# Attention and token/channel mixer on one core: k, q, v order for two groups of early loads, and projections of keys and values as two steps there

## The chip, the cores and the metric

The kernel runs on one core of one Trainium2 chip. The metric is the device time of one execution in microseconds (us). Three runs of the kernel before gave 423.52, 423.50 and 422.79 us; the median is 423.5 us. The profiled execution took 423.1 us by the same clock, and its profile spans 421.2 us from the first to the last instruction. All times within the profile count from its start.

## What is computed

The reference is a Linformer attention over batch 8, 8 heads, sequence 1024 and head width 64, whose result goes through one MLP-Mixer block. E and F are both 64 x 1024 and shorten keys and values from 1024 to 64 rows.

```python
k_proj = einsum('ks,bhsd->bhkd', E, k)
v_proj = einsum('ks,bhsd->bhkd', F, v)
attn   = softmax(q @ k_proj^T / sqrt(64))          # 1024 x 64 per head
x      = (attn @ v_proj), heads side by side       # 8 x 1024 x 512
h      = relu(x^T @ w_tok1) @ w_tok2               # token mixing, 1024 -> 256 -> 1024
u      = x + h^T
out    = u + relu(u @ w_ch1) @ w_ch2               # channel mixing, 512 -> 1536 -> 512
```

The inputs and the output are float32; the kernel works in bfloat16 and accumulates in float32.

## The kernel before

Work goes by batch. For each batch there is a **front**: the projections of keys and values, the scores, softmax and attention, then token mixing, which leaves u. After it come two **channel blocks** j = 2b and 2b + 1 of 512 rows each. A channel block has an up part (L1144, three sets m) and a down part (L1253); both use seven products where eight would be usual, so VectorE makes sums and differences beside TensorE. The front of batch b + 1 is woven into the channel blocks of batch b, so that TensorE always has channel work to do while the attention's small steps wait for ScalarE and VectorE. Batch 0 has nothing to hide behind, so its front is done by head pairs (hp = 0 to 3). Batch 1's front is done in two halves of four heads, A and B. Later batches take all eight heads at once.

Nothing of the weaving is written out by hand. Each step is a job of class Planner with an engine, a cost, what it reads and writes, the PSUM bank that it takes, and a due time (prio). plan() works through them greedily, and the instructions are then emitted in the order that it found. Each engine runs its own list in that order, and an instruction that waits holds up everything behind it on its engine. A small change in costs or due times can therefore move instructions all over the program. Where plan() expects TensorE to be idle at the start, the last loop of the kernel puts in blank matmuls on zeros (L405), which keep the array at work and compute nothing.

The steps of a front that matter here:

- load_heads (its DMA is issued at L346): one load of k, v or q for some heads from HBM, converted to bfloat16 on the way, always from GpSimd's queue. For batch 0 it is called per head pair in the order k, v, q, for batch 1 per half in the order k, v, q, from the literal "kvq".
- kv_proj (L484 and L487): 16 matmuls, eight of E with keys into rows 0 to 63 of a PSUM bank and eight of F with values into rows 64 to 127, in turns. They are one job, so none is issued ahead of the arrival of both k and v. ScalarE then copies keys (into wS, L506) and values (into vb, L506) out of the bank.
- k_transpose (L533) turns the projected keys on TensorE, with copies into kT at L544 and L549. q_transpose_pe (L581) turns q for batches 0 and 1, with the copy into qT at L589. From batch 2 on, DMA transposes on SyncE's queue do both (L516, L562).
- scores (L597), exponentials on ScalarE (L606), attend (L620), division by the row sums on VectorE (L632, L637).
- token1_pair (L1032), token2_pair (L1059, with the VectorE add at L1071) and u_transpose_pe (L1085, copies at L1091) mix tokens of batch 0. For batch 1 these are token1 (L687) and token2 (L711, with the add at L722). From batch 1 on, a DMA transpose per half of the rows makes uT from u (L759).
- The sums S at L781 need all of a uT half. With them the up part of a channel block can begin in earnest.

Loads of later batches and the transposes of u take turns. load_kv(b) ties the loads of k and of the first half of v of batch b behind the transpose of the first half of u of batch b - 2, the transpose of its second half behind that load of v, and the second load of v behind that transpose:

```python
jobs = load_group(b, "kv", first)
if second:
    tie(second, jobs[2])
    tie(jobs[3], second)
```

For b = 3 the cycle is thus: first half of u of batch 1, its transpose, loads k, k, v, transpose of the second half of u, last load v, kv_proj of batch 3.

Of the kernel before, what the change touches and what calls it, by code (L numbers as in the profile page):

```python
# [11 lines left out]
ALU = mybir.AluOpType  # L12
ACT = mybir.ActivationFunctionType
EARLY = 12.0
WHOLE = 3
TWO = 2
SUMS = 60.0
# [181 lines left out]
def kernel(  # L199
# [13 lines left out]
    nc = tc.nc  # L213
    P = 128

    B, H, S, D = q.shape
    KP = E.shape[0]
# [4 lines left out]
    NSI = S // P  # L222
# [37 lines left out]
    def bank(b):  # L260

        return banks[b.at] if b.span == 1 else psum[:, b.at : b.at + 2]
# [7 lines left out]
    k_sb, v_sb, q_sb = [tile_of([P, H, NSI, D], BF16, f"{n}_sb") for n in "kvq"]  # L270
# [11 lines left out]
    vb = tile_of([P, H, 2, D1], BF16, "vb")  # L282
# [48 lines left out]
    def act(cols, fn, **kw):  # L331
        t = cols / 1200 + 0.07
        return pl.add("ACT", t, t + 0.105, fn, **kw)
# [30 lines left out]
    for hp in range(HP):  # L364
        if hp == HP - 1:
            w1t = moe_w_tok1.rearrange("(p si) t -> p si t", p=P)
            ld(1.05, dma(wt1_sb, w1t), writes=["wt1"], prio=next(first))
        for name in "kvq":
            load_heads(0, name, 2 * hp, 2, next(first))
    w2t = moe_w_tok2.rearrange("(tc p) s -> p tc s", p=P)  # L370
    ld(1.05, dma(wt2_sb, w2t), writes=["wt2"], prio=next(first))
# [53 lines left out]
    for n, (src, dst) in enumerate(((EF[1], FT_sb), (EF[0], ET_sb))):  # L425
        b = Bank("S", full=False)

        def view(b=b):
            return bank(b).rearrange("p (si k) -> p si k", si=NSI)
# [41 lines left out]
    def kv_proj(b, h0, hn, due, block=False):  # L471
        hs = slice(h0, h0 + hn)
        hk = slice(h0 % (H // 2), h0 % (H // 2) + hn)
        heads = range(h0, h0 + hn)
        bk = Bank(stream[0], full=False)

        def view():
            return bank(bk).rearrange("p (h d) -> p h d", d=D)

        def mm(lo, hi):  # L480
            t = view()
            for si in range(lo, hi):
                a, z = si == 0, si == NSI - 1
                nc.tensor.matmul(  # L484
                    t[0:KP, 0:hn], ET_sb[:, si, :], k_sb[:, hs, si, :], start=a, stop=z
                )
                nc.tensor.matmul(  # L487
                    t[KP : 2 * KP, 0:hn], FT_sb[:, si, :], v_sb[:, hs, si, :], start=a, stop=z
                )

        cols = hn * D
        reads = ["ET", "FT"] + [(n, h) for n in "kv" for h in heads]
        pl.add(
            "PE", 8 * max(cols, 128) / 2400 + 0.22, 8 * max(cols, 128) / 2400 + 0.22,
            lambda: mm(0, NSI), reads=reads, takes=[bk], prio=due,
            after=[("vb", i, h) for i in range(2) for h in heads],
        )
        src = [lambda: view()[0:KP, 0:hn], lambda: view()[KP : 2 * KP, 0:hn]]
        if block:
            k_to = [kb[i * KP : (i + 1) * KP, hs, i, :] for i in range(2)]  # L500
        else:
            k_to = [kp[:, hk, i, :] for i in range(2)]
        v_to = [vb[i * KP : (i + 1) * KP, hs, i, 0:D] for i in range(2)]

        def copy(to, n):
            return lambda: nc.scalar.copy(out=to, in_=src[n]())  # L506

        for i in range(2):
            act(cols, copy(k_to[i], 0), writes=[("kb" if block else "kp", i, h if block else h % (H // 2)) for h in heads], uses=[bk])
        for i in (1, 0):  # L510
            act(cols, copy(v_to[i], 1), writes=[("vb", i, h) for h in heads], uses=[bk])

    def k_transpose_dma():
        sp(
# [56 lines left out]
    def q_transpose_pe(hp, due):  # L571
        bk = Bank(stream[0], full=False)

        def view():
            return bank(bk).bitcast(BF16).rearrange("p (h j s) -> p h j s", h=2, j=NJ)

        def mm():
            t = view()
            for h in range(2):
                for j in range(NJ):  # L580
                    nc.tensor.transpose(  # L581
                        t[:, h, j, :],
                        q_sb[:, 2 * hp + h, 2 * j : 2 * j + 2, :].rearrange("p s d -> p (s d)"),
                        ident,
                    )

        pe(2 * NJ, 128, mm, reads=[("q", 2 * hp), ("q", 2 * hp + 1)], takes=[bk], prio=due)
        act(
            1024, lambda: nc.scalar.copy(out=qT[:, 2 * hp : 2 * hp + 2], in_=view()),  # L589
            writes=[("qT", 2 * hp), ("qT", 2 * hp + 1)], uses=[bk],  # L590
        )
# [782 lines left out]

    for hp in range(HP):
        due = -26.0 + 3.9 * hp
        kv_proj(0, 2 * hp, 2, due)
        k_transpose(2 * hp, 2, due + 1)
        q_transpose_pe(hp, due + 1.5)
        for h in (2 * hp, 2 * hp + 1):  # L1380
            scores(h, due + 2)
        for h in (2 * hp, 2 * hp + 1):
            for half in range(2):
                attend(h, half, due + 3)
# [24 lines left out]
    def front(b, begin, end):  # L1409
        units = []  # L1410

        def unit(cost, f):
            units.append((cost, f))

        hn = H // 2 if b == 1 else H
        for i in range(H // hn):
            if b == 1:
                unit(1.9 * hn / H, lambda t, i=i: kv_proj(b, i * hn, hn, t))
                unit(0.9 * hn / H, lambda t, i=i: k_transpose(i * hn, hn, t))
            else:  # L1420
                unit(1.9, lambda t: kv_proj(b, 0, H, t - EARLY, True))
                unit(0.0, lambda t: k_transpose_dma())
            if b == 1:
                for hp in range(2 * i, 2 * i + 2):
                    unit(0.4, lambda t, hp=hp: q_transpose_pe(hp, t))
        if b + 1 < B:
            unit(0.0, lambda t: load_kv(b + 1))
        unit(0.4, lambda t: scores(0, t))
        unit(0.4, lambda t: scores(1, t))
        for h in range(H):  # L1430
            if h + 2 < H:
                unit(0.4, lambda t, h=h: scores(h + 2, t))
            if b >= WHOLE:
                unit(0.5, lambda t, h=h: attend_whole(h, t))
                continue
            for half in range(2):
                unit(0.25, lambda t, h=h, half=half: attend(h, half, t))
        if b < 2:
            for n in range(TC):
                unit(1.8, lambda t, n=n: token1(n, t))  # L1440
        else:
            unit(3.2, lambda t: token1_seven(b, t))
        if b < 3:
            for si in range(NSI):
                unit(0.55, lambda t, si=si: token2(b, si, t))
        else:
            unit(4.0, lambda t: token2_seven(b, t))
        total = sum(c for c, _ in units)
        done = 0.0
        for c, f in units:  # L1450
            f(begin + (end - begin) * done / total)
            done += c

    for hh in range(0, H, H // 2):
        for name in "kvq":
            load_heads(1, name, hh, H // 2, next(first))
    for b in range(B):
        for j in (2 * b, 2 * b + 1):
# [68 lines left out]
```

## Time and profile before

| view | what it says |
|---|---|
| time, 3 runs | 422.79 to 423.52 us, median 423.5 |
| span of the profile, mean granted TensorE clock | 421.2 us, 1.00 |
| head of the program, 0 to 36 us | TensorE is busy 31.9 us, much of it with blanks; VectorE is busy 8.84 of the 9 us from 27 to 36 |
| 47 to 75 us | TensorE is busy all 28 us |
| loads on GpSimd's queue (q0) | 34,944 packets, 45.09 MB, 54.5% of 16 engines' span |
| DMA transposes on SyncE's queue (q1) | 61,056 packets, 16.00 MB, 21.6% |

The page shows the DMA engines nearly always busy in the first 70 us (nine tenths in the slices up to there) and TensorE nearly always busy from the second slice on. The landing of a load is its issue plus the time that the tile view gives; for the loads of the first batches the table has them.

| load | issued, us | landed, us |
|---|---|---|
| batch 0, last head pair: k, v, q | 9.41, 10.66, 11.94 | 21.25, 22.53, 23.81 |
| batch 1, half A: k, v, q | 30.86, 32.22, 33.53 | 44.86, 47.45, 49.95 |
| batch 1, half B: k, v, q | 34.92, 36.77, 38.72 | 52.49, 55.03, 57.62 |
| batch 3: k, k, v, then the last v | 85.50, 86.24, 87.40, 101.96 | 92.04, 94.54, 97.14, 107.72 |

A row of the timeline or of the groups gives start, length, engine, line, operation, and the tiles written and read; in brackets is the idle time of the engine before it and what ended that.

### The profile page before, as it was taken

The numbers are of one execution on the slowest core, as the hardware profiler recorded it, in microseconds if no ns is written. First come the engines' busy times: TensorE is split into PE (matmuls) and PEld (weight loads), VectorE is DVE, ScalarE is ACT, GpSimd is POOL, SyncE is SP. The second block draws the span as 40 slices with busy tenths as digits, with TensorE's granted clock in tenths as the row PEclk, the third lists the DMA queues.
The fourth block names the chain that finished last, engine by engine and source line by source line (L and its number), as shares of the span: only waits on it lengthen the run. The fifth ranks groups of instructions, "written<-read, shape, count | busy, mean of one in ns | idle before, by whom it ended". The sixth has DMA issues, their size and how long they took to land.

```text
span 421.2 us, 9421 instructions
## 1 busy us (share of the span) xinstructions
PE 412.1 (98%) x3838; PEld 347.7 (83%) x3838; DVE 348.0 (83%) x747; ACT 231.8 (55%) x444; POOL 66.2 (16%) x104
## 2 busy tenths in 40 slices
PE   7999999999999999999999999999999999999996
PEld 3587877688788888888798888888898899988885
DVE  2359969679679798988889899898988798997685
ACT  1858884475636546564645556655646645354530
POOL 8453220022003030022103020212100000010110
PEclk9999999999999999999999999999999999999999
DMA  9999999996975989398974989999760501250223
GB/s 166 207 201 206 207 206 164 225 177 140 216 145 103 195 133 235 64 186 141 207 163 94 191 139 224 163 200 179 153 146 0 152 27 76 50 151 2 102 100 103
DMA packets 96668, 62.48 MB, mean 148 GB/s; under 512 B 62064, under 2 KB 92272, under 8 KB 96624
## 3 DMA queue, kind: packets, MB, share of 16 engines
q0 software_dynamic: 34944, 45.09, 54.5%
q1 hardware_dynamic: 61056, 16.00, 21.6%
q10 hardware_dynamic: 624, 0.79, 0.7%
q8 instruction: 30, 0.49, 0.5%
q14 instruction: 14, 0.11, 0.1%
HBM read 59.24 MB, written 16.78 MB: 180 GB/s over the span
## 4 chain that ended last, share of the span: by engine, by line
PE 91%; DVE 4%; ACT 2%; DMA 1%; issue 0%; DVEq 0%
PE psum L1253 34%; PE psum L1144 33%; PE psum L848 4%; PE psum L484 4%; PE psum L597 3%; PE psum L964 3%; PE psum L656 2%; DMA o<-in_F_dram 1%; PE psum L620 1%; DVE u L1071 1%; PE psum L736 1%; PE psum L687 1%; PE psum L581 1%; PE psum L405 1%; PE psum L711 1%; PE psum L1032 1%
## 5 line engine op out<-in xcount | busy, mean ns | idle before, releaser
L1253 PEld LDWEIGHTS <-G 128*128 128x128 bf16 x1344 | 130.6, 98 | 19.7 <-issue 1.5
L1253 PE MATMUL psum<-wc_sb,G 128*128 128x256 bf16 x768 | 102.5, 273 | 0.5 <-ACT psum L1309 0.2
L1166 ACT ACTIVATE G<-psum 128x512 bf16<-128x512 f32 x96 | 57.3, 600 | 56.0 <-PE psum L1144 55.4
L1144 PEld LDWEIGHTS <-wc_sb 128*128 128x128 bf16 x768 | 73.8, 98 | 10.9 <-issue 0.6
L1253 PE MATMUL psum<-wT,G 128*128 128x256 bf16 x576 | 77.7, 273 | 0.1
L1180 DVE TENSOR_TENSOR G<-G 128x512 bf16<-128x512 bf16 (+1 forms) x140 | 69.5, 516 | 1.0
L1144 PEld LDWEIGHTS <-wT 128*128 128x128 bf16 x576 | 55.7, 98 | 9.0 <-issue 1.2
L1144 PE MATMUL psum<-uT,wc_sb 128*128 128x256 bf16 x384 | 57.7, 273 | 0.2 <-ACT psum L1187 0.2
L1144 PE MATMUL psum<-S,wc_sb 128*128 128x256 bf16 x384 | 57.6, 273 | 0.1
L1144 PE MATMUL psum<-S,wT 128*128 128x256 bf16 x384 | 55.6, 273 | 0.4 <-DVE S L781 0.4
L1287 POOL DMA_DIRECT2D out_dram<-o x30 | 16.4, 548 | 240.2 <-DVE o L1293 125.6
L1125 DVE CUSTOM_DVE_ANT_0 G<-psum,ub 128x512 bf16<-128x512 f32 x48 | 32.9, 685 | 15.3 <-PE psum L1144 15.1
L1172 ACT COPY ua<-psum 128x512 f32<-128x512 f32 x48 | 28.2, 588 | 30.1 <-PE psum L1144 29.7
L606 ACT ACTIVATE a<-psum 128x512 bf16<-128x512 f32 x64 | 36.4, 602 | 12.4 <-PE psum L597 11.8
L1293 DVE TENSOR_TENSOR o<-psum,u 128x512 f32<-128x512 f32 x55 | 37.5, 683 | 6.4 <-PE psum L1253 6.3
L1187 ACT COPY psum<-psum 128x512 f32<-128x512 f32 x48 | 27.8, 580 | 18.9 <-DVE G L1125 9.9
L1125 DVE CUSTOM_DVE_ANT_0 G<-psum,ua 128x512 bf16<-128x512 f32 x48 | 32.7, 682 | 5.0 <-ACT ua L1172 4.6
L1172 ACT COPY ub<-psum 128x512 f32<-128x512 f32 x48 | 28.2, 588 | 7.0 <-PE psum L1144 6.3
L1144 PE MATMUL psum<-uT,wT 128*128 128x256 bf16 x192 | 28.8, 273 | 0.1
L673 DVE TENSOR_TENSOR x_sb<-psum,rdn 128x512 bf16<-128x512 f32 x40 | 27.4, 686 | 0.6
L597 PE MATMUL psum<-qT,kT 128*128 128x512 bf16 x64 | 21.5, 380 | 0.6 <-ACT kT L549 0.6
L346 POOL DMA_DIRECT2D v_sb<-in_v_dram x18 | 13.5, 749 | 50.7 <-DMA uT<-u 48.0
(108 smaller groups left out, 547.2 us busy)
## 6 DMA issues: line engine op xcount, KB each, us to landing
out_dram<-o POOLq DMA_DIRECT2D x30, 512.0 KB, 4.2
k_sb<-in_k_dram POOLq DMA_DIRECT2D x14, 512.0 KB, 8.5
v_sb<-in_v_dram POOLq DMA_DIRECT2D x14, 512.0 KB, 10.3
q_sb<-in_q_dram POOLq DMA_DIRECT2D x14, 512.0 KB, 9.9
wc_sb<-in_moe_w_ch_dram POOLq DMA_DIRECT2D x6, 256.0 KB, 12.3
wc_sb<-in_moe_w_ch_dram POOLq DMA_DIRECT2D x4, 384.0 KB, 12.3
k_sb<-in_k_dram POOLq DMA_DIRECT2D x4, 256.0 KB, 6.8
v_sb<-in_v_dram POOLq DMA_DIRECT2D x4, 256.0 KB, 7.3
```

Of the source, the lines that this page charges most:

```text
L484: nc.tensor.matmul(t[0:KP, 0:hn], ET_sb[:, si, :], k_sb[:, hs, si, :], start=a, stop=z)
L597: lambda: nc.tensor.matmul(bank(bk), kT[:, h].rearrange("p c k -> p (c k)"), qT[:, h].rearrange("p j s -> p (j s)"), start=True, stop=True,),
L606: lambda: nc.scalar.activation(out=a_t[h // 2 % 2][:, h % 2], in_=bank(bk), func=ACT.Exp, scale=scale),
L673: lambda: nc.vector.tensor_tensor(out=x_sb[:, :, h * D : (h + 1) * D].rearrange("p (n c) d -> p n c d", n=2), in0=view()[:, :, :, 0:D], in ...
L1125: nc.vector._custom_dve(TENSOR_ADD_SAT, out=out, in0=in0, in1=in1, s0=FMAX, s1=0.0)
L1144: nc.tensor.matmul(t[:, c, :], w1_of(n, dd, 2 * m + c), a_of(j, n, dd), start=(n in (1, 7) and c == 0 and dd == 0), stop=(c == 1 and dd == 1),
L1166: lambda: nc.scalar.activation(out=G[:, n, cs], in_=view(src), func=ACT.Relu),
L1172: 512, lambda: nc.scalar.copy(out=dst, in_=view("y")), writes=[(name, s % 2)],
L1180: 512 * len(both), lambda: f(out=G[:, n, c], in0=G[:, a, c], in1=G[:, b, c]), ps=False,
L1187: 512, lambda: nc.scalar.copy(out=view("y"), in_=view("x")), takes=[bk["y"]],
L1253: nc.tensor.matmul(to, G[:, G_OF[n], cc, t * P : (t + 1) * P], w2_of(n, cc), start=(n in opens and (t == 0 or alone) and cc == 0), stop=(c ...
L1293: 512, lambda: nc.vector.tensor_add(out=dst, in0=view(src), in1=u_of(sh, dh)),
```

## The change

For the last head pair of batch 0 and for half B of batch 1, the loads are issued as k, q, v, and kv_proj is replaced by two jobs from a new function one_proj: eight matmuls for keys and eight for values, each with a PSUM bank of its own and its own copies. The values' job of the head pair is due 2.5 us after the keys'; that of half B is put behind both halves' transposes in the list of due times and 2.0 us later still. All other batches, head pairs and half A keep k, v, q and kv_proj. In sum 16 matmuls of E, F in pairs become 8 and 8 for the pair, and again for the half; copies, transposes and everything else stay the same in kind and number.

```diff
+LATER = 2.0
+ORDER0 = ("kvq", "kvq", "kvq", "kqv")
+ORDER1 = ("kvq", "kqv")
+APART0 = (3,)
+APART1 = (1,)
...
-        for name in "kvq":
+        for name in ORDER0[hp]:
             load_heads(0, name, 2 * hp, 2, next(first))
...
+    def one_proj(b, h0, hn, name, due):
+
+        hs = slice(h0, h0 + hn)
+        hk = slice(h0 % (H // 2), h0 % (H // 2) + hn)
+        heads = range(h0, h0 + hn)
+        bk = Bank(stream[0], full=False)
+        k_side = name == "k"
+        rows = slice(0, KP) if k_side else slice(KP, 2 * KP)
+        w, x, wk = (ET_sb, k_sb, "ET") if k_side else (FT_sb, v_sb, "FT")
+
+        def view():
+            return bank(bk).rearrange("p (h d) -> p h d", d=D)[rows, 0:hn]
+
+        def mm():
+            for si in range(NSI):
+                nc.tensor.matmul(
+                    view(), w[:, si, :], x[:, hs, si, :], start=si == 0, stop=si == NSI - 1
+                )
+
+        cols = hn * D
+        t = 8 * max(cols, 128) / 2400 + 0.1
+        pl.add(
+            "PE", t, t, mm, reads=[wk] + [(name, h) for h in heads], takes=[bk], prio=due,
+            after=[] if k_side else [("vb", i, h) for i in range(2) for h in heads],
+        )
+        for i in (0, 1) if k_side else (1, 0):
+            if k_side:
+                to, key = kp[:, hk, i, :], [("kp", i, h % (H // 2)) for h in heads]
+            else:
+                to, key = vb[i * KP : (i + 1) * KP, hs, i, 0:D], [("vb", i, h) for h in heads]
+            act(cols, lambda to=to: nc.scalar.copy(out=to, in_=view()), writes=key, uses=[bk])
...
-        kv_proj(0, 2 * hp, 2, due)
+        if hp in APART0:
+            one_proj(0, 2 * hp, 2, "k", due)
+            one_proj(0, 2 * hp, 2, "v", due + 2.5)
+        else:
+            kv_proj(0, 2 * hp, 2, due)
...
+        late = []
...
-                unit(1.9 * hn / H, lambda t, i=i: kv_proj(b, i * hn, hn, t))
+                if i in APART1:
+                    unit(1.0 * hn / H, lambda t, i=i: one_proj(b, i * hn, hn, "k", t))
+                    late.append(lambda t, i=i: one_proj(b, i * hn, hn, "v", t))
+                else:
+                    unit(1.9 * hn / H, lambda t, i=i: kv_proj(b, i * hn, hn, t))
...
+        for f in late:
+            unit(1.0 * hn / H, lambda t, f=f: f(t + LATER))
...
-        for name in "kvq":
+        for name in ORDER1[hh // (H // 2)]:
             load_heads(1, name, hh, H // 2, next(first))
```

Because plan() orders the whole program anew, the orders of all engines differ from there on. TensorE's list has the same work but for the split projections and two blanks fewer (24 in place of 26 blank matmuls). GpSimd's list has, besides the two swaps, one store ahead of the loads of batch 3, and other small moves between stores and loads later.

## Prediction of the time after

> **What bounds the kernel now.** I read the page first, then the timelines of the engines stage by stage, and last the rows of the load and transpose queues. From the page, engines and chain:
>
> ```profile
> PE 412.1 (98%) x3838; PEld 347.7 (83%) x3838; DVE 348.0 (83%) x747; ACT 231.8 (55%) x444; POOL 66.2 (16%) x104
> ...
> PE 91%; DVE 4%; ACT 2%; DMA 1%; issue 0%; DVEq 0%
> ```
>
> TensorE ends the chain for 91% of the span. Its list is the program's length, and only two things move the end: more or fewer TensorE microseconds after the start-up, and waits of TensorE. From the starts in its timeline I add up what its matmuls need back to back: 393.8 us without blanks. Since matmuls overlap, busy time doesn't show small waits; start-to-start distances do. They lose some 11 us up to 50 us and only about 4 us in all the rest. So there is little to win later, and much that can be lost.
>
> Start-up, 22 to 36 us. ScalarE's timeline, then two rows of VectorE's:
>
> ```profile
> 22.92 0.38 ACT L1045 ACTIVATE hT_sb<-psum 128x256 bf16<-128x256 f32 x1 [0.29 <-PE psum L1032]
> 23.52 0.42 ACT L506 CAST wS<-psum 64x128 bf16<-64x128 f32 x2 [0.21 <-PE psum L487]
> 23.96 0.54 ACT L506 CAST vb<-psum 64x128 bf16<-64x128 f32 x2
> 24.53 1.01 ACT L589 COPY qT<-psum 128x1024 bf16<-128x1024 bf16 x1
> ...
> 25.70 0.26 ACT L549 CAST kT<-psum 64x128 bf16<-64x128 f32 x1
> 25.99 0.38 ACT L1045 ACTIVATE hT_sb<-psum 128x256 bf16<-128x256 f32 x1
> 26.51 1.09 ACT L606 ACTIVATE a<-psum 128x512 bf16<-128x512 f32 x2
> ```
> ```profile
> 27.16 0.69 DVE L1071 TENSOR_TENSOR u<-psum,x_sb 128x512 bf16<-128x512 f32 x1 [3.59 <-PE psum L1059]
> ...
> 35.12 0.76 DVE L781 TENSOR_TENSOR S<-uT 128x512 bf16<-128x512 bf16 x2
> ```
>
> The last head pair passes through ScalarE in a row: keys, values, q, keys again, exponentials. But from 27.16 us to the sums S at 35.12 VectorE has no gap, and TensorE's channel work proper waits for S (at 35.93). VectorE sets the end of the start-up.
>
> The projections in steady work, from TensorE's timeline:
>
> ```profile
> 55.57 0.30 PE L484 MATMUL psum<-k_sb,ET_sb 128*64 128x256 bf16 x1
> 55.57 0.30 PE L487 MATMUL psum<-v_sb,FT_sb 128*64 128x256 bf16 x1
> 55.70 0.27 PE L484 MATMUL psum<-k_sb,ET_sb 128*64 128x256 bf16 x1
> ...
> 56.57 0.39 PE L597 MATMUL psum<-qT,kT 128*128 128x512 bf16 x1
> ```
>
> Keys and values start together and pairs follow each other every 0.107 us: the second of a pair is free.
>
> The cycle of transposes and loads, SyncE's and GpSimd's timelines:
>
> ```profile
> 79.96 3.16 SPq L759 DMA_TRANSPOSE uT<-u  x1
> 83.17 2.13 SPq L562 DMA_TRANSPOSE qT<-q_sb  x1
> 97.20 1.79 SPq L759 DMA_TRANSPOSE uT<-u  x1
> ```
> ```profile
> 85.50 1.51 POOL L346 DMA_DIRECT2D k_sb<-in_k_dram  x2 [11.61 <-PE psum L620]
> 87.40 0.76 POOL L346 DMA_DIRECT2D v_sb<-in_v_dram  x1 [0.39 <-PE psum L1144]
> 100.07 0.55 POOL L1287 DMA_DIRECT2D out_dram<-o  x1 [11.91 <-DVE o L1293]
> 101.96 0.74 POOL L346 DMA_DIRECT2D v_sb<-in_v_dram  x1 [1.34 <-DMA uT<-u]
> ```
>
> Each step starts as the one before lands: the first transpose landed at 84.90, the third load at 97.14, the second transpose at 101.43, the last load at 107.72. The projection of batch 3 (L484) starts at 109.73, so the cycle has 2.0 us to spare.
>
> **What the Trainium skill says.** "TensorEngine Tiling (Array Packing)", Key Properties: different tiles of the array can execute LdWeights and Matmul in parallel. The trace agrees: 0 to 0.01 us between keys and values, one price for both. "TensorE: Matmul & The Clock Gate", Back-to-back issue gap, has N/2.4 + 2.5 ns for an isolated matmul, 109 ns for 256 columns; the trace has 109 ns at L1144, so I price a lone projection by its columns. "DMA: Bandwidth & Descriptors", Issuing engines are not separate DMA queues: all DMAs run on the same 16 engines and interleave. The trace agrees: the first loads land some 1.28 us apart although issued 0.7 us apart. A swap of order moves a landing by one such slot and saves no transfer.
>
> **The parts and their costs.**
>
> 1. *Swap of loads, last head pair.* q takes the slot of v (22.53 us) and v that of q (23.81). In the order of the changed program the keys' projection stands after the attention of the pair before, at 22.27, with k landed at 21.25. Eight matmuls at 0.055 us end at 22.7; token mixing (0.45) leads to the q transposes at 23.15, q being there. Keys' copies begin at 22.94 (0.29 after the last matmul's start, as before), the copy of qT at 23.84 in place of 24.53, kT ends at 25.27 and the scores start at 25.33: 0.69 us earlier than 26.02. The values stand at 24.2, v being there. Their two copies (0.54) and hT now stand between kT and the exponentials, which start at 26.15, 0.36 earlier. The attention follows at 26.8 and VectorE begins at 27.05 or so, not 27.16, because its list now puts both divisions first. Its work up to S is the same eight adds, two pairs of divisions and four weight differences (7.96 us). **Gain: 0.1 us**, bounds 0 and 1.28 (the whole slot).
> 2. *Two projections where one was, head pair.* 8 x 0.055 = 0.44 us more on TensorE. It stands where four blanks stood (25.03 to 26.02); two of them go. **0**; the hidden place is TensorE's wait for VectorE.
> 3. *The same for half B.* 8 x 0.107 = **+0.86 us**, amid 28 us without a gap (47 to 75). No idle time takes it. A block of pairs needs 1.00 us from 55.57 to 56.57 and 0.10 ahead, so a second changeover costs **+0.24**; bounds 0 and 0.24, as the trace has no lone projection.
> 4. *Swap of loads, half B.* k 52.49, q 55.03, v 57.62. By the order of TensorE's list keys are reached near 55.3, q transposes near 56.2, values near 59.3. None waits. Half A is reached about 1.3 us later than 47.29, so its wait for v (0.14) goes, and with it one wait for an exponential at 54.7 (0.12): **-0.26**.
> 5. *What the new order does to the cycle of batch 3.* I count TensorE's list in needed microseconds. Before, no down product of channel block 1 stands ahead of the fourth add-pair of batch 1's token2 (which ends the first half of u); after, 54 matmuls of L1253 do (5.9 us). The first half of u comes that much later, while the projection of batch 3 comes only about 2 us later: between the two stand 26.2 us of work, where 30.1 stood. The cycle itself needs, from the end of that matmul (78.7) to the last landing (107.72), 29.0 us. After, SyncE has both qT transposes ahead of uT, so the one at 83.17 no longer lies beside the loads; I give 0.6 for that. uT takes 4.3 as at 97.20, not 4.9, another 0.6. VectorE is less behind, up to 0.2. That leaves 27.6; one store now goes ahead of the loads, up to 1.3 us (a load's slot) on the same engines. I take 28.4, so TensorE loses 2.2 us, where it lost 0.9 before (31.0 us from 78.7 to 109.73 for 30.1 of work). **+1.3**, bounds +0.5 and +2.0. Everything queued behind the projection on TensorE waits with it, channel products first.
>
> Sum: -0.1 + 0.86 + 0.24 - 0.26 + 1.3 = +2.0 us on the span of 421.2. The profiled run took 423.1; against the median, 423.5 + 2.0 = **425.5 us**.
>
> **Rivals.**
>
> - *A, the cycle keeps up* (cost 5 is nil because the loads land sooner beside less traffic): 423.5 + 0.74 = 424.2. For it: 2.0 us to spare now, and three savings in the cycle that may be larger than I give. Against it: 3.9 us less work in between.
> - *B, the head pays and the kernel is not slower.* The head pair gains its whole slot of 1.28 us: S starts at 33.9, since VectorE can put off weight differences (0.34 each, four ahead of S). With A: 424.2 - 1.18 = 423.0. It decides from the point at which S starts before 34.0. Against it: the changed list has the same four differences ahead of S.
> - *C, a second late group.* For batch 6, three stores now stand between the two loads of v; for batch 7, k waits behind a store of block 8 that TensorE's list ends only 25.1 us ahead of the projection, when k, k, v, transpose and v need about 25. A loss of 2 us there on top: 427.5.
> - *D, the swap is made but nothing reads it sooner*: the order of instructions excludes this, the q transposes stand ahead of the values. It would give 423.5; no chance of its own.
>
> **How the numbers follow.** About 0.2% (0.85 us) is what a measurement of this kernel can tell from no change. Forecast with its bounds (424.4 to 427.0): 0.52. A (423.6 to 424.4): 0.20. B (422.2 to 423.6): 0.16. C (427.0 and more): 0.12. Faster than 422.65 is the lower part of B and what chance takes off the scattered waits: 0.12. Same, 422.65 to 424.35, is the rest of B and most of A: 0.24. Slower: 0.64. The range leaves out the lowest part of B and the outer part of C: 422.9 to 427.6.
>
> **What would show it.** Right: no idle TensorE at the values of half B, lone matmuls at 0.107 us; S still near 35; a wait of 1.5 to 3 us of TensorE between 104 and 115 us, ended by uT or by v of batch 3, with the first uT of batch 1 issued near 86 us in place of 79.96. Wrong: S before 34.5 (B), batch 3's last v landed before TensorE comes to it (A), or a wait of over 1 us after 230 us (C).

## The result, and the profile after

The changed kernel took 430.6 us (median of 4 runs, 429.15 to 431.02) where the kernel before took 423.5 us (median of 4, 422.79 to 424.21). The ratio is 1.0162, 95% interval 1.0132 to 1.0191. It is slower by 7.1 us; the forecast was 425.5 us, and its range ended at 427.6.

The profiled execution took 429.15 us and spans 427.3 us, 6.1 us more than the 421.2 before. In the changed file the lines moved by 5 up to the projections and by 37 behind them: the projections are L489 and L492, the transposes of u L796, the loads L351, the stores L1324, the up and down products L1181 and L1290. The projections of K or V alone are L533. From the page, the engines and the chain by engine:

```profile
PE 414.2 (97%) x3836; PEld 348.6 (82%) x3836; DVE 347.8 (81%) x747; ACT 231.7 (54%) x444; POOL 66.1 (15%) x104
...
PE 86%; DMA 5%; DVE 4%; ACT 2%; POOL 1%; issue 1%; POOLq 0%; ACTq 0%
```

TensorE's share of the chain fell from 91% to 86%, and DMA's rose from 1% to 5%. A share of the chain is not yet lost time: 9.1 us of these DMAs are a load of q in the start-up, which ended at nearly the same time (first product on S at 35.65 us, before at 35.93). The next two, 5.5 us of a load of v and 4.9 us of a transpose of u, end waits of TensorE, and its busy time grew by only 2.1 of the 6.1 us. TensorE's timeline shows where the waits are (start, length, operation, and in brackets the idle time before it and who ended it):

```profile
110.50 0.60 PE L1181 MATMUL psum<-uT,wc_sb 128*128 128x256 bf16 x4 [2.10 <-DMA uT<-u]
...
115.39 0.40 PE L489 MATMUL psum<-k_sb,ET_sb 128*64 128x512 bf16 x1
116.54 0.40 PE L492 MATMUL psum<-v_sb,FT_sb 128*64 128x512 bf16 x1 [0.74 <-DMA v_sb<-in_v_dram]
```

Counted from start to start, the first wait is 2.26 us and the second 1.04. Neither was there before. They belong to the cycle of batch 3. Its other two ends are in the timelines of SyncE and GpSimd:

```profile
86.34 22.15 SPq L796 DMA_TRANSPOSE uT<-u  x2
```
```profile
91.08 0.53 POOL L1324 DMA_DIRECT2D out_dram<-o  x1 [18.63 <-DVE rdn L669]
91.64 1.51 POOL L351 DMA_DIRECT2D k_sb<-in_k_dram  x2
93.50 0.75 POOL L351 DMA_DIRECT2D v_sb<-in_v_dram  x1 [0.35 <-PE psum L657]
94.24 0.56 POOL L1324 DMA_DIRECT2D out_dram<-o  x1
110.99 0.74 POOL L351 DMA_DIRECT2D v_sb<-in_v_dram  x1 [16.18 <-DMA uT<-u]
```

The first transpose is issued at 86.34 us, not 79.96. SyncE is then held by the second until it may go, at 105.58. Both stores of channel block 1 have moved up on GpSimd. The first is issued ahead of the loads, at 91.08; before, it came at 100.07, when the third load had landed. The second is issued right behind the third load, at 94.24; before, it came at 110.73, behind the last v. So two stores are in flight beside the three loads, where before there was none. GpSimd then waits 16.18 us for the second transpose before it can issue the last v.

At half B nothing waits, as TensorE's timeline shows:

```profile
54.82 1.06 PE L533 MATMUL psum<-k_sb,ET_sb 128*64 128x256 bf16 x8
55.82 0.62 PE L618 MATMUL psum<-ident,q_sb 128*128 128x128 bf16 x8
...
59.11 1.06 PE L533 MATMUL psum<-v_sb,FT_sb 128*64 128x256 bf16 x8
```

From the first product on S to the end the changed kernel takes 391.65 us (35.65 to 427.3), the kernel before 385.3 (35.93 to 421.2). I add up the start-to-start distances of TensorE and take off what its matmuls need:

| part of the +6.35 us | us |
|---|---|
| eight more matmul slots of half B | 0.86 |
| waits of 0.41 us for an exponential at 92.94 and 0.55 for S at 93.81 (before: 0.23 at 90.24) | 0.73 |
| cycle of batch 3, 2.26 and 1.04 | 3.30 |
| all after 120 us: many waits under 0.7 us, in other places than before | 1.0 to 1.2 |
| the rest, up to 77 us | 0.3 |

### The profile page after: what moved, and what is told of

It reads as the page before. It is cut to its first block, busy times and chain, and to the rows that moved or that the text cites. A ratio compares the mean times of both kernels' runs of the same rounds, so it can differ in the third digit from the quotient of the medians.

```text
span 427.3 us, 9409 instructions
## 1 busy us (share of the span) xinstructions
PE 414.2 (97%) x3836; PEld 348.6 (82%) x3836; DVE 347.8 (81%) x747; ACT 231.7 (54%) x444; POOL 66.1 (15%) x104
## 4 chain that ended last, share of the span: by engine, by line
PE 86%; DMA 5%; DVE 4%; ACT 2%; POOL 1%; issue 1%; POOLq 0%; ACTq 0%
PE psum L1290 32%; PE psum L1181 32%; PE psum L885 4%; PE psum L1001 3%; PE psum L634 3%; PE psum L489 2%; DMA q_sb<-in_q_dram 2%; PE psum L693 2%; DMA v_sb<-in_v_dram 1%; DMA uT<-u 1%; PE psum L657 1%; PE psum L1069 1%; DVE G L1162 1%; PE psum L724 1%; PE psum L1096 1%
## 5 line engine op out<-in xcount | busy, mean ns | idle before, releaser
L1290 PEld LDWEIGHTS <-G 128*128 128x128 bf16 x1344 | 130.5, 98 | 20.8 <-issue 1.6
L1290 PE MATMUL psum<-wc_sb,G 128*128 128x256 bf16 x768 | 102.8, 273 | 0.4 <-ACT psum L1346 0.4
L1181 PEld LDWEIGHTS <-wc_sb 128*128 128x128 bf16 x768 | 73.6, 98 | 13.0 <-issue 3.1
L1290 PE MATMUL psum<-wT,G 128*128 128x256 bf16 x576 | 77.4, 273 | 0.1
L1181 PEld LDWEIGHTS <-wT 128*128 128x128 bf16 x576 | 55.8, 98 | 9.8 <-issue 2.1
L1181 PE MATMUL psum<-uT,wc_sb 128*128 128x256 bf16 x384 | 57.7, 273 | 2.1 <-DMA uT<-u 2.1
L1181 PE MATMUL psum<-S,wc_sb 128*128 128x256 bf16 x384 | 57.6, 273 | 0.0
L1181 PE MATMUL psum<-S,wT 128*128 128x256 bf16 x384 | 54.8, 273 | 0.9 <-DVE S L818 0.9
L1324 POOL DMA_DIRECT2D out_dram<-o x30 | 16.4, 546 | 252.8 <-DVE o L1330 177.8
L1181 PE MATMUL psum<-uT,wT 128*128 128x256 bf16 x192 | 28.8, 273 | 0.6 <-DVE G L1162 0.5
L351 POOL DMA_DIRECT2D v_sb<-in_v_dram x18 | 13.5, 749 | 49.0 <-DMA uT<-u 45.5
```

Of the source, the lines that this page charges most:

```text
L1181: nc.tensor.matmul(t[:, c, :], w1_of(n, dd, 2 * m + c), a_of(j, n, dd), start=(n in (1, 7) and c == 0 and dd == 0), stop=(c == 1 and dd == 1),
L1290: nc.tensor.matmul(to, G[:, G_OF[n], cc, t * P : (t + 1) * P], w2_of(n, cc), start=(n in opens and (t == 0 or alone) and cc == 0), stop=(c ...
```

## The experiments

Fourteen kernels ran. "Order" means below what the planner made of the edit: which job stands ahead of which on each engine. It can be read from the programs without a run. For the cycle of batch 3, I use the TensorE work between the end of the first half of u of batch 1 and the projection of batch 3: 30.1 us before, 26.2 after.

| run | us | ratio to before, 95% interval |
|---|---|---|
| e1 head pair only | 429.8 | 1.0156 (1.0141 to 1.0171) |
| e2 both splits, no swap | 427.8 | 1.0121 (1.0090 to 1.0152) |
| e3 changed, block 1's down part held back | 431.05 | 1.0184 (1.0169 to 1.0200) |
| e4 changed, no turn-taking for batch 3 | 426.9 | 1.0086 (1.0071 to 1.0101) |
| e5 half B only | 428.5 | 1.0114 (1.0092 to 1.0136) |
| e6 before, matmuls split in place | 424.5 | 1.0024 (1.0009 to 1.0039) |
| e7 changed, two stores later | 443.6 | 1.0467 (1.0439 to 1.0495) |
| e8 head pair swapped, not split | 429.2 | 1.0130 (1.0111 to 1.0149) |
| e9 before, no turn-taking for batch 3 | 423.4 | 0.9998 (0.9987 to 1.0009) |
| e10 head pair split, not swapped | 423.8 | 1.0007 (0.9996 to 1.0017) |
| e11 changed, two stores from SyncE | 430.3 | 1.0162 (1.0143 to 1.0181) |
| e12 before, belief of half B +0.83 us | 428.5 | 1.0117 (1.0091 to 1.0142) |
| e13 before, belief of head pair +0.41 us | 426.1 | 1.0057 (1.0039 to 1.0074) |
| e14 before, belief of half B +0.30 us | 428.9 | 1.0143 (1.0106 to 1.0179) |

### e1 to e4: work, order or turns

e1 takes half B's edits out of the changed kernel:

```diff
-ORDER1 = ("kvq", "kqv")
+ORDER1 = ("kvq", "kvq")
-APART1 = (1,)
+APART1 = ()
```

> Only the head pair of batch 0 is swapped and split; half B of batch 1 is loaded and projected as before. TensorE's needed work rises by 0.43 us alone, but TensorE's order is that of the changed kernel: 54 down products of channel block 1 stand ahead of the end of the first half of u of batch 1, and only 26.2 us of work lie between that end and the projection of batch 3 (before: 30.1). Theory 'order' (the projection of batch 3 waits for its loads because these 26 us are too few for the chain transpose, loads, transpose, load): nearly all of the loss, 428.5 to 430 us, with TensorE idle for 2 to 4 us between 104 and 118 us. Rival 'work' (the 48 additional matmuls and their changes of tile cost more than worked out): a third of the loss, about 425.5 us, and no such idle time.

429.8 us: nearly the whole loss with a third of the additional TensorE work (0.43 of 1.29 us; no matmuls are added, they only lose the partner that ran beside them), as "order" said. The first transpose went out at 86.95 us and TensorE waited 2.51 us for the second. A price came on top in the profiled execution that no theory had: the granted clock. The windows of this run give the stretch, its length, then each engine's busy time with its instructions (TensorE first), and behind these the clock (third column from the end). Two windows of the changed kernel follow.

```profile
108.02:111.43 3.41, 1.06 (x11) 0.81 (x9) 1.18 (x3) 0.37 (x1) 0.00 (x0) 1.00 0.83 121
111.43:114.84 3.41, 3.41 (x17) 2.45 (x17) 3.41 (x9) 0.89 (x2) 2.22 (x3) 0.50 0.33 46
```
```profile
106.50:109.91 3.41, 1.90 (x17) 1.43 (x15) 1.96 (x4) 1.23 (x3) 0.00 (x0) 1.00 1.10 150
109.91:113.33 3.42, 2.83 (x26) 2.53 (x26) 2.85 (x8) 1.62 (x4) 2.22 (x3) 1.00 0.14 21
```

After its wait of 2.51 us TensorE ran 3.41 us at half of its clock, with 17 matmuls where the changed kernel has 33 in the 3.5 us after its wait. That is another 1.7 us (half of 3.41) behind the wait. The Trainium skill, "TensorE: Matmul & The Clock Gate", What's actually happening, describes this: half rate after an idle window of about 3.4 us, in a window that runs freely. The traces agree on the half rate, on its length and on the window: in each of them the clock changes only at points whole multiples of 3.41 us apart (in e1 at 12.45, 111.43 and 114.84 us, in the changed kernel at 4.10, 7.51 and 10.93). They do not agree on how idle the window must be: 1.06 us of work in it did not keep the clock up in e1, nor 1.37 in e11. In the changed kernel the point at 109.91 cuts the wait of 2.26 us in two; the window with its first part has 1.90 us of work, and the clock stayed at 1.00. So the place of a wait between these points decides with its length. Where the border lies is not shown: the clock fell after 1.97 us of work in e3 and stayed after 1.97 in e8, and in the start-up it fell after windows with 1.7 to 2.4 us.

e2 keeps both splits and puts all loads back to k, v, q:

```diff
-ORDER0 = ("kvq", "kvq", "kvq", "kqv")
-ORDER1 = ("kvq", "kqv")
+ORDER0 = ("kvq", "kvq", "kvq", "kvq")
+ORDER1 = ("kvq", "kvq")
```

> Both splits, all loads in the order k, v, q as before: all the additional TensorE work (1.29 us, and two more changes of tile), but the down products of block 1 stay behind the first half of u of batch 1, with 28.4 us of work up to the projection of batch 3. Theory 'order': 424.8 to 425.6 us, no wait for batch 3 above 1 us. Rival 'work': the whole loss, 430 us or more. Rival 'load order' (the swap of q and v is what costs): 423.5 to 425 us, as 'order' says, so this run parts only 'work' from the other two.

427.8 us hits neither theory. No wait for batch 3's loads is left (the largest in that stretch is 0.58 us, for ScalarE), so that part of "order" holds. Yet 4.6 us were lost, 3.5 more than the split costs by itself (e6), in small waits: 0.87 us at 173.4, 0.62 at 88.9, 0.58 at 109.3 and many under 0.5.

e3 makes the planner keep block 1's down products behind the first half of u, as they stood before:

```diff
+        if (b, si) == (1, 3):
+            for d in down1:
+                d.deps.add(job)
```

> The changed kernel with one dependency more in the planner: the down products of channel block 1 come after the fourth product of token2 of batch 1. Loads and splits are those of the changed kernel, the same TensorE work; the work up to the projection of batch 3 is 27.7 us and the stores ahead of its loads are two, not three. Theory 'order': 424.8 to 426.5 us, the idle time between 104 and 118 us under 1.5 us. Rivals 'work' and 'load order': 430 us, as the changed kernel.

431.05 us: my theory failed here. The cycle was mended (three loads in 12.28 us, no wait of TensorE for them above 0.25), but the price moved. TensorE's list now brought the attention steps of batch 1 faster than VectorE could divide: VectorE was busy without a gap from 66 to 76.6 us. TensorE's timeline:

```profile
74.03 0.39 PE L657 MATMUL psum<-vb,a 128*128 128x130 bf16 x4 [0.46 <-DVE x_sb L674]
74.76 0.27 PE L657 MATMUL psum<-vb,a 128*128 128x130 bf16 x2 [0.35 <-DVE x_sb L674]
...
76.59 0.58 PE L489 MATMUL psum<-k_sb,ET_sb 128*64 128x512 bf16 x1 [0.68 <-DVE x_sb L674]
```

Counted from start to start, it lost some 3.7 us between 72 and 77 us, some 3.1 of them for x_sb, and here too the clock fell, to 0.50 from 76.04 to 79.45. A repaired chain in a new order can open another that is dearer.

e4 leaves the order alone and lets the second transpose of u of batch 1 go when its u is there:

```diff
-        if j in tied and tied[j] is not shown:
+        if j in tied and tied[j] is not shown and j is not turned_u.get((1, 1)):
```

> The changed kernel, same order on TensorE and GpSimd, but the second transpose of u of batch 1 doesn't wait for the three loads of batch 3 ahead of it; it goes when its u is there. Theory 'order' with the turn-taking as the limb that hurts: the two waits of 2.26 and 1.04 us at 110.5 and 116.5 us shrink to under 1 us in sum, 427 to 428 us. Rival 'transfers' (the loads and stores are as long as they are whatever the turns, because the queues are full): the last v comes as late as before, 430 to 431 us.

426.9 us, by the medians 3.7 less than the changed kernel and just below what was expected. In the profiled executions, from the first product on S to the end, it is 2.9 us less (388.7 against 391.65). The two waits of 3.3 us lie between. SyncE's timeline now has both transposes within 5 us, and TensorE comes to the projection without waiting:

```profile
86.80 4.81 SPq L796 DMA_TRANSPOSE uT<-u  x2
```
```profile
113.06 0.60 PE L1181 MATMUL psum<-S,wc_sb 128*128 128x256 bf16 x4
113.59 0.40 PE L489 MATMUL psum<-k_sb,ET_sb 128*64 128x512 bf16 x1
113.59 0.40 PE L492 MATMUL psum<-v_sb,FT_sb 128*64 128x512 bf16 x1
```

The cycle thus costs the changed kernel 2.9 to 3.7 us. This is shown, not argued: in the traces of both, every engine has the same instructions in the same order.

### e5 to e8: the parts, the price of the split, the stores

e5 has half B's edits alone (ORDER0 all "kvq", APART0 empty).

> Only half B of batch 1 is swapped and split; the last head pair of batch 0 is as before. 0.86 us more of TensorE work; the down products of block 1 stay behind the first half of u of batch 1, with 29.2 us of work up to the projection of batch 3. Theory 'order': no wait for batch 3 above 0.7 us, 424.2 to 425.5 us, plus what an order that is new elsewhere scatters in waits under 1 us each (0 to 2 us as the runs of head pair alone and of both splits showed). Rival 'half B is the costly part': 428 us or more.

428.5 us: the number is the rival's, and nothing of the loss is batch 3's. But it isn't the split of half B that is dear (e6 gives its price): TensorE's list and the landings disagree there. What ORDER1 asks isn't what happens: loads are emitted in the order in which the planner believes their buffers free, and half B's buffers are the last head pairs' of batch 0. In e5 half B's loads landed as k, v, q (52.2, 54.8, 57.3), although ORDER1 says k, q, v. In e1 they landed as k, q, v, although ORDER1 says k, v, q, since the head pair had been swapped. TensorE's list expected the other sequence. Here it meets q, which lands last:

```profile
57.39 1.07 PE L618 MATMUL psum<-ident,q_sb 128*128 128x128 bf16 x16 [1.51 <-DMA q_sb<-in_q_dram]
```

This wait is 1.5 of the 5.1 us lost. What remains beyond the price of the split is smaller waits; e12, below, explains one of them, at 173.9 us.

e6 is the kernel before with its own lists. Only inside kv_proj, for those two groups, the matmuls are sorted:

```diff
+            if (b, h0) in ((0, 2 * (HP - 1)), (1, H // 2)):
+                steps.sort(key=lambda x: x[1])
+            for si, s in steps:
```

> The kernel before, its loads, its plan and its order unchanged on every engine; only within the projections of the last head pair of batch 0 and of half B of batch 1 the 8 matmuls of K come first and then the 8 of V, so none run side by side. This is the price of the split by itself, 1.29 us of TensorE work. Theory 'order': 423.9 to 424.9 us (0.86 us of half B and up to 0.3 us for its changes of tile; the head pair's 0.43 us lies in a stretch where TensorE has idle time). Rival 'work': 426 us or more.

424.5 us against 423.35, so +1.1 us: "order" was right, and this is the price of splitting: 1.29 us of TensorE work, of which the head pair's 0.43 can hide.

That is the median. The 18 executions spread from 423.2 to 428.5 us, and the profiled one is the longest. Its trace has a wait that the profile of the kernel before doesn't have, although the lists differ only in the sorted matmuls:

```profile
87.09 0.82 PE L598 MATMUL psum<-qT,kT 128*128 128x512 bf16 x3 [2.35 <-DMA kT<-kb]
```

The transposes of batch 2 took longer in this execution, and kT landed at 87.04 us. Before, it landed at 83.04, only 0.4 us ahead of its first reader (83.44). Counted from start to start the wait is 2.51 us, and the clock fell behind it as in e1 (0.50 from 87.98 to 91.40). A second execution took 428.4 us. So an unlucky execution can lose some 4 us with no change of order, and a single trace can mislead; the medians are what the comparisons rest on.

e7 emits block 1's stores behind the third load of batch 3:

```diff
     plan = pl.plan()
+    held = [j for j in plan if j in late_stores]
+    plan = [j for j in plan if j not in late_stores]
+    at = max(n for n, j in enumerate(plan) if j in third)
+    plan[at + 1 : at + 1] = held
```

> The changed kernel, but the two stores of channel block 1 are issued behind the first three loads of batch 3 instead of ahead of and between them. Theory 'the stores stretch the loads' (15.0 us from the first transpose's landing to the third load's in the changed kernel, 12.2 us before, with one store less): the three loads take 12 to 13 us, the waits at 110.5 and 116.5 us shrink by 2 to 2.7 us in sum, 428 to 428.8 us. Rival 'the loads are slow for another cause': 15 us again, 430 to 431 us.

This kernel leaves something out: a store now stands in the program ahead of the last sum added into its rows, which then misses from the output. That sum on VectorE waited 14.8 us for the store, and TensorE behind it, so 443.6 us says nothing on the question. One reading can be used: the three loads landed 13.28 us after the transpose, not 14.93 (expected were 12 to 13).

e8 swaps the head pair's loads and splits nothing.

> Only the order of loads of the last head pair of batch 0 (k, q, v), nothing split: no more TensorE work than before. The planner leaves block 1 behind the first half of u of batch 1; 28.4 us of work up to the projection of batch 3. Theory 'order': no wait for batch 3 above 1 us, 423 to 425.5 us (0 to 2.3 us of scattered waits). Rival 'the swap of the head pair is what costs': 428 us or more.

429.2 us with no additional work at all. The number is the rival's, but not its reason: the trace shows a wait for half B's v, whose load landed last while TensorE's list met it early, then 1.24 us at 110.4 for ScalarE and the small waits of e2.

```profile
55.83 0.30 PE L489 MATMUL psum<-k_sb,ET_sb 128*64 128x256 bf16 x1
57.57 0.27 PE L492 MATMUL psum<-v_sb,FT_sb 128*64 128x256 bf16 x1 [1.44 <-DMA v_sb<-in_v_dram]
```

### e9 to e11: two controls, and who issues the stores

e9 is e4's edit on the kernel before.

> The kernel before with the edit that took 3.7 us off the changed kernel: the second transpose of u of batch 1 doesn't wait for the three loads of batch 3. In the kernel before 30.1 us of TensorE's work lie between the first half of u and the projection of batch 3, and the last v landed 2.0 us ahead of that projection. Theory 'order' (the chain of transposes and loads costs only what it exceeds the work beside it): nothing to gain, 422.8 to 423.9 us. Rival 'the turn-taking costs in itself, whatever the order': 421 us or less.

423.4 us, no difference: the turn-taking costs nothing in the order of before. As a test of the cycle's length it is weak, since the cycle got no shorter: the second transpose, issued earlier, landed at 101.04 us (before: 101.43) and the last v at 107.64 (before: 107.72). That a shorter one would gain nothing there is argued from its 2.0 us to spare, not shown.

e10 splits the head pair alone (APART0 = (3,), everything else as before).

> Only the split of the last head pair of batch 0; all loads as before, GpSimd's list the same line by line, and TensorE's order differs little: 30.1 us of work up to the projection of batch 3. 0.43 us more of TensorE work, in a stretch where TensorE has idle time. Theory 'a new order is what costs, not the edit': 423.2 to 424.2 us. Rival 'the split of the head pair costs in itself': 425 us or more.

423.8 us against 423.5: none that can be measured. This edit left GpSimd's list as it was and moved little on TensorE.

e11 issues block 1's two stores from SyncE:

```diff
-            queue = (nc.sync if sh else nc.scalar) if last else nc.gpsimd
+            queue = (nc.sync if sh else nc.scalar) if last else nc.sync if j == 1 else nc.gpsimd
```

> The changed kernel with the two stores of channel block 1 issued by SyncE, so that no store stands in GpSimd's list among the first three loads of batch 3; TensorE's order is that of the changed kernel. Theory 'the place in GpSimd's list is what stretches the loads' (15 us from the first transpose to the third load's landing with stores among them, 11.9 to 12.4 us in the runs with none): 12 to 13 us, TensorE's wait at 110 us shrinks by 2 us or more, 427.5 to 429 us. Rival 'the bytes are what stretches them, whoever issues': 14.5 us or more, 430 to 431 us.

430.3 us. The rival is right. The cycle in the runs, from the landings of each DMA (us):

| | first uT issued, landed | third load landed, after uT | second uT landed | last v landed |
|---|---|---|---|---|
| before | 79.96, 84.90 | 97.14, 12.24 | 101.43 | 107.72 |
| changed | 86.34, 90.59 | 105.52, 14.93 | 110.46 | 116.50 |
| e2, no store among the loads | 83.73, 88.09 | 100.01, 11.92 | 104.30 | 110.24 |
| e4, stores among them | 86.80, 91.04 | 106.29, 15.25 | 94.05 | 110.24 |
| e11, stores from SyncE | 86.96, 91.21 | 106.16, 14.95 | 111.02 | 117.20 |
| e12, no store among them | 84.09, 88.72 | 100.75, 12.03 | 105.05 | 111.17 |

With one store of 512 KB issued just ahead of the three loads and one among or right behind them, the loads need about 15 us, without stores about 12, whichever engine issues the stores: 2.7 to 3.0 us for the two. That agrees with the Trainium skill, "DMA: Bandwidth & Descriptors", Issuing engines are not separate DMA queues, by which the issuer makes no difference. Where the stores stand does make one: with both right behind the third load it was 13.28 us (e7), and with a single one issued later, at 94.27 us, 12.07 (e13, below). For the loads the landings are 2.5 us apart, so a store costs somewhat over half of a load; a load writes as many bytes (512 KB of bfloat16), but reads twice as many (float32).

### e12 to e14: the same instructions in another order

After e8, the suspicion was that the edit hardly matters. e12 adds one term to the duration by which the planner reckons with half B's projection. No instruction is changed:

```diff
-            "PE", 8 * max(cols, 128) / 2400 + 0.22, 8 * max(cols, 128) / 2400 + 0.22,
+            "PE", *[8 * max(cols, 128) / 2400 + 0.22 + (0.83 if (b, h0) == (1, 4) else 0)] * 2,
```

> The kernel before, nothing swapped and nothing split: only the planner believes that the projection of half B takes 0.83 us longer, about what the split costs. The instructions are those of before, to the last one; their order is new from the middle of batch 2's work on, and from batch 3 on it is the order of the runs of both splits, of half B and of the head pair's swap (5,500 to 5,700 of TensorE's last instructions agree one by one). Theory 'a new order is what costs, not the edit': those runs lost 2.2 to 2.4 us more than before in the last 300 us of work, and up to 1 us around the projection of batch 3, so 425.5 to 427 us. Rival 'the edits cost by themselves': 423.5 us, as before.

428.5 us: 5.4 us lost by order alone, more than expected. It isn't that any new build loses: e9 has the order of before, e10 nearly so, and both keep its time. The largest wait in the trace of e12 is for kT. On SyncE both transposes of q now stand ahead of that of k (before: q, k, u, q), and kT lands at 87.07 in place of 83.04. SyncE's and TensorE's timelines:

```profile
73.23 9.45 SPq L562 DMA_TRANSPOSE qT<-q_sb  x2
82.77 1.26 SPq L516 DMA_TRANSPOSE kT<-kb  x1
```
```profile
87.11 0.60 PE L597 MATMUL psum<-qT,kT 128*128 128x512 bf16 x2 [1.72 <-DMA kT<-kb]
...
89.81 0.81 PE L1253 MATMUL psum<-wc_sb,G 128*128 128x256 bf16 x6 [0.45 <-DVE wait L1293]
...
174.35 0.38 PE L964 MATMUL psum<-hT_sb,wt_sb 128*128 128x256 bf16 x2 [0.70 <-DVE a L994]
```

How much of the wait for kT is the order's is open: e6 had it once with the order of before, and e13 and e14, whose SyncE has the transposes in e12's order there, got kT at 84.96 and 85.40 and did not wait for it. The wait at 174.35 (0.87 us from start to start) is the one that e2 has at 173.4, e5 at 173.9 and e8 at 174.5: their orders are the same from batch 3 on. So e2, e5 and e8 lost there by their order, not by their edits.

e13 and e14 move other beliefs: 0.41 for (0, 6), and 0.3 for (1, 4).

> The kernel before with the same instructions; the planner believes that the projection of the last head pair of batch 0 takes 0.41 us longer. The first 1,550 and the last 3,780 of TensorE's 7,663 instructions stand as before, the middle (about 70 to 210 us) is new, with 30.5 us of work up to the projection of batch 3. Theory 'each stretch of new order costs there, by the chains it leaves too little work beside': nothing lost in the last 210 us, no wait for batch 3, 424 to 426 us. Rival 'any plan but the one before costs the same 4 to 6 us, wherever it differs': 427.5 us or more.

426.1 us, just above the upper edge. The profiled execution is one of the two fastest (424.7), so its trace shows less than half of the loss. That loss is local: from the projection of batch 7 to the end e13 took 121.8 us, the kernel before 122.1. In the new stretch TensorE waits 1.17 us for batch 3's last v at 112.45 and 0.58 for S at 107.96. More work beside the cycle (30.5 us) did not save it, because the cycle grew as well, from 29.0 us to 33.7 (78.7 to 112.41): SyncE has both transposes of q and that of k ahead of uT, which it issues at 82.96 us in place of 79.96, and a store issued at 103.94 stands beside the last v, which takes 7.6 us to land instead of 5.8.

> The kernel before with the same instructions; the planner believes that the projection of half B takes 0.3 us longer instead of 0.83. All of the order from 70 us on is new, and it is another one than that of the belief of 0.83 us. 29.2 us of work up to the projection of batch 3. Theory 'a new order is what costs': 425.5 to 428 us. Rival 'the size of the belief sets the loss': 0.36 of 5.3 us, 425 us. Rival 'that one order was an unlucky draw': 423 to 424.5 us.

428.9 us, above the expectation. Another order, the same loss, in other places (1.67 us for VectorE at 240.9, 0.87 for ScalarE at 377.1, 0.80 for S at 108.3). The size of the belief doesn't set it, and e12 isn't the only such order that loses.

## Why the prediction was wrong

The direction and the place were right, the size was not. Point by point:

1. **Swap in the head pair, -0.1.** Nothing of a gain is seen. S began at 34.84 us against 35.12, but this execution began its first projection 0.57 us earlier (8.82 against 9.39), so the start-up took 0.29 more. From the first projection to the first product on S it is 26.8 us after and 26.5 before, and runs whose start-up is that of before (e9, e12, e13, e14) have 27.3 to 28.1. A size below 1 us can't be told here.
2. **Split of the head pair, 0.** Right (e10).
3. **Split of half B, +0.86 and +0.24.** Right: lone matmuls at 0.107 us, and +1.1 us in place (e6).
4. **Half B's loads, -0.26.** None waited, as said, but by luck: the swap of the head pair alone brings the order k, q, v, through the buffers (e1), and ORDER1 alone doesn't (e5).
5. **Cycle of batch 3, +1.3.** This step failed in its size. The first transpose was issued at 86.34 (forecast near 86), and TensorE waited between 104 and 117 us for uT and v. But the cycle needed 31.1 us (85.4 to 116.50) where 28.4 was taken. Two stores lay beside the loads, not one, for 2.7 us in place of 0.8: the prediction counts the store that moves ahead of the loads, but not the other, which now stands ready behind the third load (issued at 94.24); before, the store in that place waited for its sum until 100.07. The second transpose took 4.88 us, not 4.23; the second store was still in flight until 106.81. The relief of 0.6 for the moved qT didn't come as such: loads without stores took 11.8 to 12.4 us in the other runs against 12.24. With the cycle removed, 2.9 to 3.7 us are gone (e4), which lies beyond the bound of +2.0.

The second fault lies in the sum itself. It priced the new order in one place and everywhere else at zero, though front and prediction both said that instructions move all over the program. Of the 7.1 us, 1.1 is the split (e6) and 2.9 to 3.7 the cycle (e4), taken each from its own run. The remaining 2.3 to 3.1 I put down to the new order's other waits. Their kind is shown by e12 and e14, which lose 5 us and more with before's own instructions; which of the small ones in the changed kernel adds how much wasn't tried one by one, and up to 1.5 us of the loss is in no trace. Rivals A, B and C did not occur: the last v wasn't there in time, S was no earlier, and after 230 us no wait exceeded 0.7 us.

What stays open: the three unprofiled runs of the changed kernel took 1.5 to 1.9 us more than the profiled one. A fall of the clock after the wait of 2.3 us, as in e1 and e11, would be about that much, and the same wait may meet it in one execution and not in another. The mean clocks on record don't settle it. A fall takes 0.004 off the mean; the profiled execution has 0.996, with its one fall in the start-up, and the others have 0.991, 0.996 and 0.996. So one of them had a fall more, and where those of the other two lay is not known. Nor is it known why before's order is better than the nine others that ran (the changed kernel, e1, e2, e3, e5, e8, e12, e13, e14); no kernel here beats it.

## What to carry to other kernels

Where a greedy planner writes the program, run a placebo ahead of judging an edit: change only a duration that the planner believes in. If the placebo costs as much as the edit, the order was measured, and the edit must be priced inside the old order (as in e6). For a cycle of transfers, compare its length with the work beside it, and count every transfer in flight with it and every transpose queued ahead, whichever engine issues it; in these runs only the excess cost, and a wait above 2 us may cost again through the clock. Compare medians of several executions: a place with only 0.4 us to spare, and the clock behind it, made the profiled execution of e6 some 4 us longer than its median.

## What the runs showed of the hardware

- The clock changed only at points whole multiples of 3.41 us apart, and each fall in mid-program was to half; it lasted 3.41 us in e1, e3, e6 and e11. It followed windows between two such points with 1.06 us of TensorE work (e1, e6), 1.37 (e11) and 1.97 (e3). It did not follow 1.90 us (the changed kernel), 1.92 (e14), 1.97 (e8) and 2.23 (e12). A single wait of 2.2 to 2.5 us was thus enough where it lay within one window.
- A transpose issued behind two loads did not pay in itself: in e9 the second uT, issued at 86.54 us in place of 97.20, took 14.5 us to land (101.04; alone 4.2), and the third load landed at 100.05, not 97.14. In e4, issued ahead of the loads, it took 4.3 us.
- A lone block of matmuls on half of the columns costs 0.09 us of changeover ahead of it and about 0.14 in and behind it (the changed kernel, blocks at 54.82 and 59.11 us).
